# T5-bias attention with a maxout FFN: the values' load waits for the bias row's store, the second pass of batch 0 reuses the first pass's tiles and puts scores ahead of AV, the first FFN chunk runs weight by weight, and all loads are issued in written order

## The chip, the cores and the metric

The kernel runs on one core of one Trainium2 chip. The time is device microseconds of that core, the median over several runs. The core has five engines that run side by side: TensorE (PE, matmuls; its weight loads are shown as PEld), VectorE (DVE), ScalarE (ACT), GpSimd (POOL) and SyncE (SP). Sixteen DMA engines move data. In this kernel SP and ACT issue some transfers and POOL issues the rest; every transfer that changes f32 to bf16 on its way is POOL's.

## The reference

Two stages in sequence. Shapes: 8 batches, 8 heads, 576 positions, head size 64; model width 512, FFN width 768.

```python
scores = scale * q @ k.T                       # per batch and head, 576 x 576
scores = scores + bias_table[bucket(|i - j|)]  # 32 buckets, distances above 128 share one
attn   = exp(scores - max) / sum
x      = (attn @ v) laid out as 4608 tokens x 512
h      = maximum(maximum(x @ w1, x @ w2), x @ w3)
out    = h @ w_out                             # 4608 x 512, f32
```

## The kernel before

**Tiles.** Positions are four key tiles of 128 (`KT`) and a tail of 64. Heads go in pairs `hp` (four pairs). For a pair, `visit(qT, kT, e4, c)` makes the scores of 256 queries (`c` is 0 or 1) against all four key tiles: two PSUM tiles `sc` (two buffers of `ps_s`, L528), eight matmuls, and two `exp` on ACT (L522) of 128x1024 each into `e4`. `left_keys` (tile `sct`) and `left_queries` (tile `scq`) make the scores of the tail into `el`. The bias enters as a factor exp(bias): `times_band` (L516) multiplies `e4` on DVE by a band `hank`; `times_bandt` and `times_band_left` do the same for `el`. `attend(b, hp, e4, el, half)` multiplies with the values (`vx`, `vt`) into the PSUM tile `a` and gives back `quotients`, a reciprocal and a product on DVE (L608, L609) that write `x_sb`.

**The bias band.** `spread_bias` (L278) spreads the 32-entry table to a row per head with one matmul, takes exp on ACT, and stores the row to DRAM (`w_dr`, L287, queue of ACT). `load_hank` (L293, queue of SP) reads it back 128 times, one element further per partition, which gives the band. It waits for the store.

**Loads.** Batch 0 comes partly through f32 staging (`load_32`, `k32`, `q32`, queues of SP and ACT, cast by `cast_keys`), the rest from POOL (`load_main` L143, `load_tail` L160). Values are loaded by `load_v`. Then come the three weights `w_bf` (L660), the q and k of batch 1 in a packed form (`load_packed` L205, rearranged by `spread_packed` L210), the values of batch 1, `wo_bf` (L674), and `load_qk(2)` (L167). From batch 2 on q and k are turned by DMA transposes on SP (`transposes`, L447), handed out one position tile at a time by `next(crossbar)`; batches 0 and 1 are turned by PE (`first_transposes`, `more_transposes`, `second_transposes`).

**Order.** `inorder` fixes an instruction's place among those of its engine. Matmuls, DVE's work and SP's transfers are so fixed; POOL's loads are only from batch 3 on (`in_turn`, L133). PE runs through what is written, so an instruction that waits holds up all matmuls behind it.

**Batch 0 in two passes.** The first pass (L688) makes the scores of queries 0 to 255 for the four pairs; `late` collects the `attend` calls. The second pass (L719) makes those of queries 256 to 511 into new `e4` and `el` tiles, and between them takes attends from `late` (`next_late`). From batch 1 on (L768) each pair makes two visits, each followed by one attend of earlier work and by FFN work.

**FFN.** `add_ffn` cuts a chunk of tokens into portions, which `fill(target)` puts between the attention's matmuls: whole portions while their sum is at most `target`, and always one at least. A portion's number counts units of one matmul of 512 columns: 4 for a product of 128 FFN columns with one weight (`first`, `second`, `third` for w1, w2, w3), 6 for an `output` of 128 tokens. Tokens 0 to 255 and 256 to 511 are two small chunks, the rest chunks of 512. `x_transposes` (PE and ACT) bring batch 0's `x_sb` to `xT`, which the FFN reads; later batches use a DMA transpose (L619). A last output of a chunk (`rest`) is joined to the next chunk's first portion.

Of the kernel before, what the change touches and what calls it, by code (L numbers as in the profile page):

```python
# [39 lines left out]
def kernel(  # L40
# [77 lines left out]
    def constants(i):  # L118
        inorder(nc.vector.memset(ktail[i][:], 0.0))
        if i == 0:  # L120
            inorder(nc.vector.memset(qtail[i][:], 0.0))
        inorder(nc.vector.memset(vt[i][:], 0.0))
        inorder(nc.vector.memset(vx[i][:, :, :, D:AW], 1.0))
        for par in range(2):
            inorder(nc.vector.memset(vt[i][64 * par : 64 * par + 64, :, par, D:AW], 1.0))
# [7 lines left out]
    def in_turn(b, load):  # L133
        return inorder(load) if b > 2 else load

    def load_main(src, b, h0, h1, dst, t0=0, t1=KT):
        x = main_part(src, b)
        if h1 - h0 < KT:
            for h in range(h0, h1):
                nc.gpsimd.dma_start(out=dst[:, :, h, :], in_=x[:, :, h, :])  # L140
        else:
            for t in range(t0, t1):
                in_turn(b, nc.gpsimd.dma_start(out=dst[:, t, h0:h1, :], in_=x[:, t, h0:h1, :]))  # L143

# [16 lines left out]

    def load_qk(b, behind=None):

        loads = []
        for t in range(KT):
            for src, dst in zip((q, k), batch[b]):
                loads.append(in_turn(b, nc.gpsimd.dma_start(out=dst[:, t], in_=main_part(src, b)[:, t])))  # L167
        for src, dst in ((q, q_diag), (k, k_diag)):
            for par in range(2):
                load = nc.gpsimd.dma_start(out=dst(b, par, 0, H), in_=tail_part(src, b, 0, H, par))  # L170
                loads.append(in_turn(b, load))
        if behind:
            for load in loads:
                tc.add_manual_dep(
                    load.ins, behind.ins.name,
                    mybir.DependencyInfo(mybir.DependencyClass.Sync, mybir.DependencyReason.DATA),
                    reason="these loads go behind the result's transposes",
                )

    def load_v(b, h0, h1):  # L180
        load_main(v, b, h0, h1, vx[b % 2][:, :, :, 0:D])
        load_tail(v, b, h0, h1, v_diag)

# [36 lines left out]
    nc.gpsimd.dma_start(out=table[:], in_=bias_table)  # L220
    ident = const.tile([P, P], BF16, name="ident")
    make_identity(nc, ident[:])
    load_32(k, 0, k32, nc.scalar)
    load_32(k, 1, k32, nc.scalar)
    for h in range(2, KT):
        load_32(q, h, q32, nc.scalar, 2)
    nc.scalar.preload_act_table_set("natural_log_exp_and_others")
    for h in range(2):
        load_32(q, h, q32, nc.sync, 2)
    for h in range(2, H):  # L230
        load_32(k, h, k32, nc.sync)
# [6 lines left out]
    nc.gpsimd.iota(ids[:, 0:NW], pattern=[[1, NW]], base=0, channel_multiplier=0)  # L238
    nc.gpsimd.iota(ids[:, NW:], pattern=[[0, 1]], base=0, channel_multiplier=1)
# [4 lines left out]
    inorder(nc.vector.memset(qtail[1][:], 0.0))  # L244
# [13 lines left out]
    constants(1)  # L258
# [4 lines left out]
    load_v(0, 0, H)  # L263
# [8 lines left out]
    for _ in range(8):  # L272
        mm(warm[:, 0:CH], lhsT=zeros[:, 0:P], rhs=zeros[:])

    act_copy(batch[0][0][:, 0:2, 0:2, :], q32[:, :, 0:2, :])
    w_sb = stage.tile([H, WL], BF16, name="w_sb")

    def spread_bias():  # L278
        spread = ps_a.tile([H, NW], F32, tag="a", name="spread")
        mm(spread[:], lhsT=table[:], rhs=pick[:, 0:NW])  # L280
        negc = stage.tile([H, 1], F32, name="negc")
        inorder(nc.vector.tensor_scalar(
            out=negc[:], in0=spread[:, HALF:], scalar1=-1.0, scalar2=None, op0=ALU.mult,
        ))
        for out_, in_ in ((w_sb[:, HALF:], spread[:]), (w_sb[:, 0:HALF], spread[:, HALF:0:-1])):
            inorder(nc.scalar.activation(out=out_, in_=in_, func=ACTF.Exp, bias=negc[:]))
        inorder(nc.scalar.dma_start(out=w_dr[:], in_=w_sb[:]))  # L287
# [27 lines left out]
    def ffn(t0, nt, last):  # L315
# [13 lines left out]

        def bank(name):  # L330
            return ps_f.tile([P, CH], F32, tag="ff", name=name)

        def first(fb):
            ps0 = ps_a.tile([P, CH], F32, tag="a", name="ps0") if last else bank("ps0")
            product(ps0, fb, 0)
            st[fb]["m0"] = ffnw.tile([P, CH], BF16, tag="m0", name="m0")
            nc.scalar.activation(out=st[fb]["m0"][:], in_=ps0, func=ACTF.Copy)  # L337

        def second(fb):
            ps1 = ps_s.tile([P, 2 * CH], F32, tag="sc", name="ps1")[:, 0:CH] if last else bank("ps1")  # L340
            product(ps1, fb, 1)
            m = st[fb]["m"] = ffnw.tile([P, CH], BF16, tag="m", name="m")
            inorder(nc.vector.tensor_tensor(out=m[:], in0=ps1, in1=st[fb]["m0"][:], op=ALU.max))  # L343

        def third(fb):
            ps2 = bank("ps2")
            product(ps2, fb, 2)
            inorder(nc.vector.tensor_tensor(  # L348
                out=hT[:, fb * CH : fb * CH + CH], in0=ps2, in1=st[fb]["m"][:], op=ALU.max
            ))  # L350
# [36 lines left out]
        if per == 1:  # L387
            portions = [[f[0], m[0]]]
            for fb in range(1, n_fb):
                portions.append([g[fb - 1], f[fb], m[fb]])  # L390
            portions.append([g[-1], (0, None), o[0]])
        else:
            portions = []
            for fb in range(n_fb):
                portions += [[f[fb]], [m[fb], g[fb]]]
            portions.append(o[:1])
        if len(o) > 2:
            portions.append(o[1:3])
        return portions, o[-1:]

    pending, rest, stores = [], [], []
# [6 lines left out]
    def add_ffn(t0, nt, last=False):  # L408
        portions, left = ffn(t0, nt, last)
        portions[0] = rest + portions[0]  # L410
        rest[:] = left
        pending.extend((sum(n for n, _ in p), [fn for _, fn in p]) for p in portions)
# [237 lines left out]
    cast_keys(0)  # L650
    spread_bias()
    first_transposes(0)
    for h0 in (0, KT):
        load_hank(h0, h0 + KT)
# [3 lines left out]
    for i, wk in enumerate((moe_w1, moe_w2, moe_w3)):  # L658
        wb = const.tile([P, DCH, d_ff], BF16, name=f"w{i}_bf")
        nc.gpsimd.dma_start(out=wb[:], in_=wk.rearrange("(c p) f -> p c f", p=P))  # L660
        w_bf.append(wb)
    batch[1] = load_tiles()
    wo_bf = const.tile([P, FCH, d_model], BF16, name="wo_bf")

    def load_second():
# [6 lines left out]
        spread_packed(0, nc.gpsimd)  # L672
        load_v(1, 0, H)
        nc.gpsimd.dma_start(out=wo_bf[:], in_=moe_w_out.rearrange("(c p) m -> p c m", p=P))  # L674

    def bands(hp):
        for t in range(KT):
            times_band(hp, first_e[hp], t, 0, QS, inorder)
# [7 lines left out]
    first_e, lefts = [], []  # L686
    x_sb[0] = x_tile()
    for hp in range(HP):  # L688
        qT, kT = (x[:, hp, :] for x in qk[0])
        e4, el = e_tiles()  # L690
        first_e.append(e4)
        visit(qT, kT, e4, 0, (lambda: first_transposes(hp + 1)) if 0 < hp < HP - 1 else None)
        if hp == HP - 1:
            more_transposes(0)
        if hp == 0:
# [5 lines left out]
        if hp == HP - 1:  # L701
            bands(0)
            bands(1)
# [14 lines left out]

    for hp in range(HP):  # L719
        qT, kT = (x[:, hp, :] for x in qk[0])  # L720
        e4, el = e_tiles()
        visit(qT, kT, e4, 1, (lambda: more_transposes(hp + 1)) if hp + 1 < HP else None)
        if hp == 0:
            bands(HP - 2)
            bands(HP - 1)
        if hp == 1:
            x_transposes(0, 0)
        if hp == 2:
            x_transposes(2, 0)
            x_transposes(3, 0)  # L730
            add_ffn(0, QS)
        quotients = next_late()
# [7 lines left out]
        def late_bands():  # L740
            for t in range(KT):
                times_band(hp, e4, t, QS, QM, inorder)

        if hp < 2:
            quotients()
            keys()
            if hp == 1:
                x_transposes(1, 0)
            quotients = next_late()
            queries()  # L750
            quotients()
            if hp == 0:
                make_bandt()
            late_bands()
            products(hp, el)
        else:
            if hp == HP - 1:
                batch[2] = load_tiles()
                load_qk(2)
                x_transposes(0, 1)  # L760
            quotients()
            late_bands()
            fill(8, keys, queries, *([lambda: second_transposes(qk[1], 0)] if hp == HP - 1 else []))
            products(hp, el)
        late.append(lambda hp=hp, e4=e4, el=el: attend(0, hp, e4, el, 1))

    turned = [lambda hp=hp: x_transposes(hp, 1) for hp in range(1, HP)]
    for b, hp in [(b, hp) for b in range(1, B) for hp in range(HP)]:  # L768
# [19 lines left out]
        if turned:  # L788
            turned.pop(0)()
# [14 lines left out]
        if turned:  # L804
            turned.pop(0)()
# [5 lines left out]
        if hp == 1:  # L811
# [62 lines left out]
```

The softmax here doesn't subtract the row's maximum and nothing guards it: scores larger than these inputs give would overflow.

## Time and profile before

| | |
|---|---|
| median of 6 runs | 326.43 us (323.98 to 326.67) |
| the profiled execution's own time | 326.29 us |
| its span in the profile | 324.5 us |
| busy, share of the span | PE 307.2 us (95%), DVE 215.9 us (67%), ACT 201.9 us (62%), POOL 112.6 us (35%) |
| granted TensorE clock, mean | 0.989 |
| stretch 16.40 to 20.80 us | PE busy 0.02 of 4.40 us |
| stretch 20.80 to 25.80 us | PE busy 4.99 of 5.00 us, clock 0.50 |
| batch 1's matmuls, 38.0 to 66.5 us | PE busy 27.81, ACT 24.29, DVE 22.54 of 28.50 us |
| batch 4's matmuls, 130.9 to 164.8 us | PE busy 33.58 of 33.90 us |

The span begins with the first and ends with the last instruction; the run's time is 1.8 us longer. Busy time of PE is modelled from pipelined matmuls, so gaps of a tenth of a microsecond don't show. L94 is the helper that issues every matmul, and L110 and L107 are the helpers for copies on DVE and ACT, so those groups are told apart by their tiles. For a DMA the profile has the time at which an engine issued it and the time from issue to landing.

### The profile page before, as it was taken

The numbers are of one execution on the slowest core, as the hardware profiler recorded it, in microseconds if no ns is written. First come the engines' busy times: TensorE is split into PE (matmuls) and PEld (weight loads), VectorE is DVE, ScalarE is ACT, GpSimd is POOL, SyncE is SP. The second block draws the span as 40 slices with busy tenths as digits, with TensorE's granted clock in tenths as the row PEclk, the third lists the DMA queues.
The fourth block names the chain that finished last, engine by engine and source line by source line (L and its number), as shares of the span: only waits on it lengthen the run. The fifth ranks groups of instructions, "written<-read, shape, count | busy, mean of one in ns | idle before, by whom it ended". The sixth has DMA issues, their size and how long they took to land.

```text
span 324.5 us, 7978 instructions
## 1 busy us (share of the span) xinstructions
PE 307.2 (95%) x3191; PEld 176.0 (54%) x3232; DVE 215.9 (67%) x537; ACT 201.9 (62%) x274; POOL 112.6 (35%) x151
## 2 busy tenths in 40 slices
PE   7747999999999999999999999999999999999995
PEld 2335776776545555555555555555555554444442
DVE  6466978777676766676667766777667675454452
ACT  3938898898676667766777677667776651121221
POOL 8941977209747761195009610500000000000000
PEclk9969999999999999999999999999999999999999
DMA  9999999959999999999989999996032003301103
GB/s 168 177 207 198 150 161 141 166 128 126 179 167 152 156 177 174 125 123 168 202 81 122 168 209 87 104 210 115 1 71 101 34 3 75 130 0 65 67 0 129
DMA packets 165541, 40.72 MB, mean 125 GB/s; under 512 B 155384, under 2 KB 161024, under 8 KB 165504
## 3 DMA queue, kind: packets, MB, share of 16 engines
q0 software_dynamic: 103904, 16.66, 75.7%
q1 hardware_dynamic: 59840, 23.08, 39.3%
q10 hardware_dynamic: 1760, 0.47, 0.6%
q8 instruction: 25, 0.41, 0.5%
q14 instruction: 12, 0.10, 0.1%
HBM read 35.39 MB, written 9.45 MB: 138 GB/s over the span
## 4 chain that ended last, share of the span: by engine, by line
PE 81%; DMA 6%; ACT 5%; POOL 3%; issue 2%; DVE 2%; SPq 0%; POOLq 0%; ACTq 0%
PE ps L94 39%; PE a L94 14%; PE pso L94 13%; PE sc L94 9%; ACT e L522 4%; DMA kT<-k_sb 3%; PE sct L94 2%; DMA vt<-in_v_dram 2%; PE scq L94 2%; POOL vx L143 1%; POOL q_sb L143 1%; PE tp L97 1%; DMA out_dram<-osb 1%; ACT el L522 1%; DVE e L516 0%
## 5 line engine op out<-in xcount | busy, mean ns | idle before, releaser
L94 PE MATMUL ps<-xT,w_bf 128*128 128x512 bf16 (+1 forms) x692 | 152.5, 357 | 1.5
L522 ACT ACTIVATE e<-sc 128x1024 bf16<-128x1024 f32 x128 | 124.3, 1026 | 25.0 <-PE sc L94 24.4
L94 PEld LDWEIGHTS <-w_bf 128*128 128x128 bf16 x720 | 65.6, 98 | 56.8 <-issue 1.5
L516 DVE TENSOR_TENSOR e<-e,hank 128x512 bf16<-128x512 bf16 (+2 forms) x136 | 59.7, 467 | 27.6 <-ACT e L522 24.9
L337 ACT ACTIVATE m<-ps 128x512 bf16<-128x512 f32 x54 | 32.3, 598 | 65.7 <-PE ps L94 63.3
L343 DVE TENSOR_TENSOR m<-ps,m 128x512 bf16<-128x512 f32 x54 | 37.3, 690 | 46.0 <-ACT el L522 24.6
L94 PEld LDWEIGHTS <-kT 64*128 64x128 bf16 (+1 forms) x704 | 35.5, 95 | 39.4 <-issue 22.7
L94 PE MATMUL pso<-wo_bf,hT 128*128 128x512 bf16 (+2 forms) x209 | 50.2, 373 | 0.7
L94 PE MATMUL a<-vx,e 128*128 128x65 bf16 x1024 | 46.1, 195 | 0.0
L94 PE MATMUL a<-vt,el 128*128 128x130 bf16 (+1 forms) x192 | 40.1, 216 | 4.4 <-DMA vt<-in_v_dram 4.4
L94 PE MATMUL sc<-qT,kT 64*128 64x256 bf16 x512 | 41.1, 274 | 2.7 <-DVE kT L110 1.0
L94 PEld LDWEIGHTS <-e 128*128 128x128 bf16 x1024 | 41.8, 99 | 1.0 <-issue 0.2
L143 POOL DMA_DIRECT2D vx<-in_v_dram x32 | 28.4, 896 | 38.2 <-PE a L94 33.8
L348 DVE TENSOR_TENSOR hT<-ps,m 128x512 bf16<-128x512 f32 x54 | 37.0, 685 | 5.1 <-PE ps L94 3.3
L609 DVE TENSOR_TENSOR x_sb<-a,rd 128x256 bf16<-128x256 f32 (+1 forms) x64 | 31.4, 491 | 2.2
L94 PEld LDWEIGHTS <-el 128*128 128x128 bf16 x448 | 24.3, 97 | 15.7 <-issue 10.1
L110 DVE COPY osb<-pso 128x512 f32<-128x512 f32 (+1 forms) x33 | 22.7, 687 | 13.4 <-PE pso L94 10.1
L94 PEld LDWEIGHTS <-hT 128*128 128x128 bf16 x222 | 20.2, 98 | 20.6 <-DVE hT L348 0.4
L167 POOL DMA_DIRECT2D q_sb<-in_q_dram x24 | 22.1, 922 | 16.5 <-DVE x_sb L609 14.3
L522 ACT ACTIVATE el<-sct 128x640 bf16<-128x640 f32 (+2 forms) x36 | 23.2, 646 | 5.7 <-PE sct L94 5.1
L167 POOL DMA_DIRECT2D k_sb<-in_k_dram x24 | 22.0, 917 | 7.5 <-DMA vx<-in_v_dram 5.9
L522 ACT ACTIVATE el<-scq 128x512 bf16<-128x512 f32 x32 | 19.0, 595 | 6.6 <-PE scq L94 6.6
(69 smaller groups left out, 168.8 us busy)
## 6 DMA issues: line engine op xcount, KB each, us to landing
out_dram<-osb SPq DMA_DIRECT2D x35, 256.0 KB, 3.2
vx<-in_v_dram POOLq DMA_DIRECT2D x32, 128.0 KB, 6.3
q_sb<-in_q_dram POOLq DMA_DIRECT2D x26, 128.0 KB, 8.6
k_sb<-in_k_dram POOLq DMA_DIRECT2D x24, 128.0 KB, 8.8
w_bf<-in_moe_w_dram POOLq DMA_DIRECT2D x3, 768.0 KB, 14.1
xT<-in_k_dram SPq DMA_DIRECT2D x6, 128.0 KB, 4.4
hank<-w_dr SPq DMA_DIRECT2D x2, 384.0 KB, 7.4
wo_bf<-in_moe_w_out_dram POOLq DMA_DIRECT2D x1, 768.0 KB, 8.4
```

The costliest lines, as they stand in the source:

```text
L94: inorder(nc.tensor.matmul(*args, **kw))
L97: inorder(nc.tensor.transpose(*args))
L110: return inorder(nc.vector.tensor_copy(out_, in_))
L143: in_turn(b, nc.gpsimd.dma_start(out=dst[:, t, h0:h1, :], in_=x[:, t, h0:h1, :]))
L167: loads.append(in_turn(b, nc.gpsimd.dma_start(out=dst[:, t], in_=main_part(src, b)[:, t])))
L337: nc.scalar.activation(out=st[fb]["m0"][:], in_=ps0, func=ACTF.Copy)
L343: inorder(nc.vector.tensor_tensor(out=m[:], in0=ps1, in1=st[fb]["m0"][:], op=ALU.max))
L348: inorder(nc.vector.tensor_tensor(out=hT[:, fb * CH : fb * CH + CH], in0=ps2, in1=st[fb]["m"][:], op=ALU.max))
L516: put(nc.vector.tensor_tensor(out=e4[:, t, :, lo:hi], in0=e4[:, t, :, lo:hi], in1=hank[:, 2 * hp : 2 * hp + 2, c0:c1][:, :, ::-1], op=ALU. ...
L522: nc.scalar.activation(out=out_, in_=in_, func=ACTF.Exp, scale=inv_sqrt_d)
L609: divided[b, hp, half] = inorder(nc.vector.tensor_tensor(out=x_sb[b][:, 2 * half : 2 * half + n, P * hp : P * hp + P].rearrange("p t (h d) ...
```

## The change

- `load_v(0)` waits for the store of the bias row (`go_behind`), and stands behind `spread_bias` in POOL's order.
- All loads of POOL are in written order. The written order is now: q and k of batch 0, values of batch 0, w1, first packed q and k of batch 1 with their tails, w2, `spread_packed(0)`, the other packed q and k, values of batch 1, w3, `w_out`.
- The start: the bias table goes over SP's queue instead of POOL's, the identity is made by two POOL instructions behind the `iota`s, two clears move from DVE to POOL, the first casts are all DVE's and take one head each, 6 warming matmuls stand where 8 did and one more after the first transposes, and `constants(1)` moves behind the third pair of the first pass.
- The second pass of batch 0 uses `e4` and `el` of the first. Pairs 0 and 1 have all their scores (visit, keys, queries) ahead of the first attends, with extra `keep_warm` matmuls; the bands of the first pass move from its end into pairs 0 and 1 of the second. Attends start at the end of pair 1. Three attends of the second half are made in the second pass, where two were.
- The small FFN chunks go by weights: all products with w1, then with w2; those with w3 and the outputs of tokens 0 to 255 follow the second small chunk's w1 and w2 products. Every product is a portion of its own. The intermediate maxima are kept in `hT`. `fill(4)` is called three times in the second pass where `fill(8)` was called twice.
- In batch 1 the second small chunk is added in pair 0, where it was pair 1; `x_transposes` are taken two at a time.

```diff
+            return [
                 in_turn(b, nc.gpsimd.dma_start(out=dst[:, t, h0:h1, :], in_=x[:, t, h0:h1, :]))
+                for t in range(t0, t1)
+            ]
...
+    def go_behind(loads, other, reason):
+        for load in loads:
+            tc.add_manual_dep(load.ins, other.ins.name, ...)
...
+    def load_v(b, h0, h1, behind=None):
+        loads = load_main(v, b, h0, h1, vx[b % 2][:, :, :, 0:D])
         load_tail(v, b, h0, h1, v_diag)
+        go_behind(loads if behind else [], behind, "the bias row is on its way to memory alone")
...
-    nc.gpsimd.dma_start(out=table[:], in_=bias_table)
...
+    inorder(nc.sync.dma_start(out=table[:], in_=bias_table))
...
+    inorder(nc.gpsimd.memset(ident[:], 0.0))
+    inorder(nc.gpsimd.affine_select(out=ident[:], in_=ident[:], ...
+    for x in (qtail, ktail):
+        inorder(nc.gpsimd.memset(x[1][:], 0.0))
...
-            st[fb]["m0"] = ffnw.tile([P, CH], BF16, tag="m0", name="m0")
+            st[fb]["m0"] = part(fb) if t0 < CH else ffnw.tile([P, CH], BF16, tag="m0", name="m0")[:]
...
+        if per > 1:
+            return [[x] for x in f + m], [[x] for x in g + o]
...
+        if t0 == 0:
+            third[:] = left
+        elif t0 < CH:
+            portions += third + left[:-1]
+            rest[:] = left[-1]
+        else:
+            portions[0] = rest + portions[0]
+            rest[:] = left[0]
...
-    cast_keys(0)
-    spread_bias()
+    dve_copy(batch[0][1][:, :, 0, :], k32[:, :, 0, :])
+    dve_copy(batch[0][0][:, 0:2, 0:2, :], q32[:, :, 0:2, :])
+    dve_copy(batch[0][1][:, :, 1, :], k32[:, :, 1, :])
+    row = spread_bias()
+    load_v(0, 0, H, row)
...
+                load_weights(1, moe_w2)
+                spread_packed(0, nc.gpsimd)
         load_v(1, 0, H)
+        load_weights(2, moe_w3)
...
         if hp == HP - 1:
             more_transposes(0)
+            more_transposes(1)
...
+        e4, el = first[hp]
+        visit(qT, kT, e4, 1, (lambda: more_transposes(hp + 2)) if hp + 2 < HP else None)
...
+        if hp < 2:
+            bands(2 * hp)
+            bands(2 * hp + 1)
+            keys()
+            keep_warm()
+            queries()
+            keep_warm()
         if hp == 1:
+            next_late()()
+            next_late()()
         if hp == 2:
+            for half in range(2):
+                next_late()()
+                x_transposes(half, 0)
+            keys()
+            queries()
             x_transposes(2, 0)
             x_transposes(3, 0)
             add_ffn(0, QS)
+            make_bandt()
+            late_bands(0)
+            fill(4)
+        if hp == 3:
+            batch[2] = load_tiles()
+            load_qk(2)
+            late_bands(1)
+            next_late()()
+            fill(4, keys)
             queries()
+            late_bands(2)
+            next_late()()
+            fill(4, lambda: second_transposes(qk[1], 0))
         late.append(lambda hp=hp, e4=e4, el=el: attend(0, hp, e4, el, 1))
+    late_bands(3)
+    next_late()()
...
-        if hp == 1:
+        if hp == (b > 1):
             add_ffn((b - 1) * CH if b > 1 else QS, CH if b > 1 else QS)
```

## The prediction

> **What bounds the kernel now.** I read the stretches first, then PE's waits, then the chain, then SP's and POOL's timelines. The stretches (microseconds from A to B; busy time and count per engine, clock, DMA share, GB/s):
>
> ```profile
> 9.00:12.00 3.00, 2.55 (x30) 1.24 (x27) 1.53 (x5) 2.82 (x6) 3.00 (x4) 1.00 2.34 151
> 16.40:20.80 4.40, 0.02 (x2) 0.02 (x1) 3.34 (x12) 1.69 (x2) 1.67 (x3) 0.79 1.59 200
> 20.80:25.80 5.00, 4.99 (x58) 3.62 (x59) 3.40 (x14) 2.35 (x4) 2.19 (x4) 0.50 1.16 210
> 33.00:35.00 2.00, 2.00 (x44) 1.68 (x43) 1.97 (x6) 1.94 (x4) 1.97 (x4) 1.00 0.97 119
> 38.00:66.50 28.50, 27.81 (x414) 21.09 (x417) 22.54 (x62) 24.29 (x36) 16.43 (x22) 1.00 1.97 161
> 66.50:97.10 30.60, 30.03 (x371) 19.07 (x374) 22.41 (x57) 23.80 (x32) 18.20 (x23) 1.00 1.54 144
> 130.90:164.80 33.90, 33.58 (x364) 18.75 (x370) 23.66 (x56) 23.64 (x31) 14.28 (x18) 1.00 1.73 152
> ```
>
> From batch 2 on PE sets the pace. Batch 4 has 96 FFN units of 0.216 us (eight matmuls of 256 columns, four units, stand with 0.87 us in the chain), 20.7 us, which leaves 13.2 us for its attention. Time is lost only before about 66 us. Where, the waits and the chain say:
>
> ```profile
> PE a L94 <- DMA vt<-in_v_dram: 4.4, 1, 4.4
> ...
> 12.19 0.58 POOL vt L160
> 12.77 7.90 DMA vt<-in_v_dram
> 20.68 0.14 issue
> 20.81 1.25 PE a L94 x18
> ```
>
> The first attend stands ahead of the second pass's work and waits 4.4 us for the values; then TensorE runs at half clock for 5 us, in which the 58 matmuls would have needed about half the time. The second pass starts late by some 4.4 + 2 us. The other thing to see is when batch 2's operands come. SP's timeline, SP's longest wait, PE's timeline and POOL's:
>
> ```profile
> 48.77 1.29 SPq L447 DMA_TRANSPOSE qT<-q_sb  x1
> ...
> 58.52 1.22 SPq L447 DMA_TRANSPOSE kT<-k_sb  x1
> ...
> SPq L447 <- DMA q_sb<-in_q_dram: 40.4, 4, 37.2
> ...
> 66.47 0.61 PE L94 MATMUL sc<-qT,kT 64*128 64x256 bf16 x8
> ...
> 28.48 0.83 POOL L205 DMA_DIRECT2D xT<-in_k_dram  x1 [3.19 <-DMA w_bf<-in_moe_w_dram]
> 32.44 0.82 POOL L205 DMA_DIRECT2D xT<-in_q_dram  x1 [3.13 <-DMA w_bf<-in_moe_w_dram]
> ...
> 39.30 0.89 POOL L674 DMA_DIRECT2D wo_bf<-in_moe_w_out_dram  x1
> 40.12 0.95 POOL L167 DMA_DIRECT2D q_sb<-in_q_dram  x1
> ```
>
> SP sits from 11.4 to 48.77 until the first q of batch 2 has landed, and then issues ten transposes back to back. The last key tile's (58.52) takes 7.3 us to land: 65.8. PE reads it in the second half of the visit at 66.47, at about 66.7. So batch 2 can start only about 0.9 us earlier than it does, however early PE gets there, unless its loads come earlier. They stand last in POOL's line: batch 0, V, three weights, batch 1, `w_out`, then they.
>
> **What the Trainium skill says.** "TensorE: Matmul & The Clock Gate", section "The HAM clock gate": an idle window returns the array to half clock. The trace agrees: idle from 16.4, half clock until 25.8. "DMA: Bandwidth & Descriptors", section "Queues, rings and completion order": each DMA engine takes turns between the queues that have work. The trace agrees: the band's read on SP's queue (issued 10.47, landed 17.3) and the values on POOL's share the engines. Same page, section "Anatomy of one DMA": a wait happens on the issuing sequencer before dispatch. So V's new wait holds all POOL work behind it; no run shows that yet.
>
> **The change, part by part.**
>
> *Start.* The table landed 3.6 us after its issue at 1.29, 4.9, and the spread began at 5.02. On SP it is third, issued about 1.7; with the neighbours' 2.5 us it lands at 4.2 to 4.5. No `constants(1)` (0.84 us) stands ahead of the first casts, but those wait for k's second head (1.28 + 3.5 = 4.8). I take 0.6 us earlier for row and first scores. POOL loses a DMA issue (0.66) and gains two clears of 128x512, unseen there: 0.2 us each (scaled down from DVE's 0.27) to 0.8 (POOL's copy of this size is 0.74). Taking 0.5, its loads start within 0.4 us of 2.80. The key tails already made PE wait at 9.86, so the first pass gains little: it ends on ACT at 18.0 (before: 18.09).
>
> *V behind the row.* The row left at 7.35 and landed at 10.4, 3.1 us later; 0.6 earlier is about 9.7, against V's first issue at 8.55. Six issues (4 x 0.9 + 2 x 0.65 = 4.9 us) follow. Queued behind on POOL: w1 and everything else. The q and k loads fill the DMA to about 11, so I put the hole at 1.1 us (0 to 2): V lands near 21.8, the band near 16.7.
>
> *Scores ahead of AV.* Pairs 0 and 1 of the second pass cost ACT 2 x (2.0 + 0.45 + 0.6) = 6.1 us, from 18.0 to 24, so V is needed only at about 23; there the 4.4 us go. The clock dip then costs nothing, as ACT sets the pace. Whole second pass: ACT 12.2, four `xT` copies 1.4, three w1 copies 1.8, half of `second_transposes` 0.8, together 16.2 us. DVE: twelve band products 3.7, their second-half twins 3.8, tails 2.0, seven quotients 4.5, `bandt` 1.0, copies 1.5, together 16.5 us from 16.7. Neither is free to follow the other exactly; with 2 us of friction it ends at 36. Before it ended at 37.98, with one attend (1.0 us) fewer. The four new `keep_warm` matmuls (0.22 us each, 0.9 us on PE) are hidden by ACT's pace; were PE the slower engine there, they would cost that.
>
> *Batch 1.* PE: attention 13.2, less one attend 1.0, three `second_transposes` 1.65, four `xT` turns 0.5, 60 FFN units 13.0, together 27.3 us; before, 52 units and 26.5 us took 28.5. I take 28.5: PE is ready for batch 2 at 64.5, 2 us earlier than before.
>
> *Loads in order.* The same bytes stand ahead of batch 2's loads. Against: the hole of 1.1 us. For: before, the DMA ran thin twice because POOL issued late, in 33.0 to 35.0 (119 GB/s, against 190 before it) and in 41 to 42 (93 GB/s against 175): 0.75 + 0.5 us. The first came of the packed load that waited for w3 (32.44); in the new order packed loads stand ahead of w3 and w2's 3.9 us cover `spread_packed`'s 1.4. So batch 2's loads move by -0.2 us, (-1.5 to +1.5), and batch 2 can start 0.9 + 0.2 = 1.1 us earlier. PE has 2 us. Of the two the later counts: **-1.0 us**, the rest becomes a new wait at batch 2.
>
> *FFN ahead.* I played the portions through both versions. Units done at the start of batch 2: 64 before, 72 after; at the start of batch 3: 140 and 152; the difference of 12 then stays until the attention ends. Batch 2 carries four more (+0.86 us), and its end has 0.38 us of DMA wait less, as PE waited that long at 97.12 for keys. Behind batch 3 there are 12 fewer: **-2.6 us**.
>
> *Tokens of batch 1.* In batch 2 the first 512-token chunk starts one visit earlier: at about 78.3 on the old clock, where it started at 81.27. It needs the fourth of five DMA transposes that SP issues from 69.30 to 77.30; with 5.3 us to landing that is 79.2. **+0.8 us** (0 to 1.5).
>
> Moves without cost: maxima kept in `hT` (the same writes); the small chunk's w2 and w3 (their first use is behind 36 and 48 us, they land by about 32 and 44); shared `e4` tiles (the queries differ).
>
> Sum: -1.0 + 0.86 - 0.38 - 2.6 + 0.8 = -2.3 us. The profiled run took 326.29, so 324.0 (span 322.2); it lies at the median of 326.43, and I say **324.1 us**.
>
> **Rivals.**
>
> 1. *Batch 2's loads come with PE, early.* The holes at 33 and 41 us close and V's wait makes none: loads 2 us earlier, PE 3 us earlier if the second pass has no friction. Then -2.9 instead of -1.0: 322.2. For: DMA is then full all through. Against: ACT and DVE both nearly full.
> 2. *The operands land when they did.* Hole of 2 us, nothing gained later: batch 2 starts at 66.5, and with 1.5 us for tokens the sum is 0 + 0.48 - 2.6 + 1.5 = -0.6: 325.8, no change.
> 3. *The new wait halves the clock (slower).* PE waits 2 to 4 us at batch 2's first visit as it did for V. The half clock after that wait lasted 6.8 us in the trace's clock record, 1.8 of it idle. In batch 2 PE sets the pace and nothing hides it: up to 6.8/2 = 3.4 us. With rival 2: -0.6 + 3.4 = +2.8: 329.2. It decides once batch 2 starts no earlier than before and the halved stretch is over 4.5 us long. For: the same idle did it at 16.4. Against: PE's wait would be shorter than those 4.4 us by my sum.
>
> That V's wait on the row leaves the band no earlier, because k and q fill the DMA until 11 anyway, is possible and changes the sum by less than 0.5 us.
>
> **How the numbers follow.** A difference under 0.5% (1.6 us) can't be told from none. My case 0.45, own range 322.8 to 325.4; rival 1 0.18; rival 2 0.20; rival 3 0.17. Faster is below 324.8: 0.36 of mine and all of rival 1, 0.54. Same: 0.09 of mine, 0.17 of rival 2, 0.03 of rival 3, 0.29. Slower: 0.03 of rival 2 and 0.14 of rival 3, 0.17. For 8 in 10 the range reaches from 321.0 into rival 3, to 328.6.
>
> **What would show it.** Right: no wait of attend for V over 1 us; batch 1's first visit near 36; a PE wait of 0.5 to 2 us for DMA transposes at batch 2's first visit near 65.5; the later visits some 2 us earlier than before. Wrong: V landing after 24, with PE idle behind it; the first q of batch 2 landing before 47 or after 50; a clock of half after 60 us; a PE wait for `xT` over 1.5 us near 78.

## The result, and the profile after

The changed kernel takes 329.03 us (median of 18 runs, 325.77 to 334.24) against 326.3 for the kernel before (median of 39 runs here, where the six above gave 326.43): ratio 1.0083, 95% interval 1.0060 to 1.0106. It is slower by 2.7 us; 324.1 was predicted, and the range of 321.0 to 328.6 ends below the median. One of the 18 runs, that of 334.24 us at a mean clock of 0.983, was in a slower state and is left out of the ratio; without it the median is 328.64. The profiled execution took 328.12 us with a span of 326.3 (before 326.29 and 324.5), so its 1.8 us are what the trace can explain; the medians lie 0.5 to 0.9 further apart.

The stretches of the kernel after, in the columns used before (A:B and length; busy time and count of PE, PEld, DVE, ACT, POOL; clock, DMA share, GB/s):

```profile
16.40:20.80 4.40, 2.73 (x27) 1.51 (x29) 2.37 (x9) 4.31 (x8) 3.52 (x6) 1.00 1.96 174
20.80:25.80 5.00, 4.11 (x84) 3.17 (x81) 3.44 (x12) 3.77 (x6) 1.83 (x3) 1.00 1.43 194
38.00:66.50 28.50, 26.95 (x359) 20.42 (x361) 21.34 (x56) 23.07 (x35) 13.42 (x17) 1.00 1.78 175
66.50:97.10 30.60, 28.83 (x350) 17.61 (x354) 21.14 (x53) 21.85 (x27) 18.30 (x23) 1.00 1.59 138
130.90:164.80 33.90, 32.72 (x352) 17.96 (x355) 22.67 (x54) 22.58 (x29) 14.26 (x18) 1.00 1.44 138
```

The hole at 16.4 and the half clock behind it are gone in this execution: the first two rows have clock 1.00 and 111 matmuls where there were 60. The later rows pay for it: PE is idle for 1.55, 1.77 and 1.18 us in these stretches, where before it was for 0.69, 0.57 and 0.32. What PE waits for, by the operation released and its releaser (total us, times, longest):

```profile
PE ps L93 <- ACT xT L106: 2.2, 3, 0.9
...
PE ps L93 <- DMA xT<-x_sb: 1.2, 1, 1.2
PE sc L93 <- DMA kT<-k_sb: 1.0, 1, 1.0
PE sct L93 <- DMA kT<-ktail: 0.9, 1, 0.9
```

There is no wait for V at all. In its place stand three waits for DMA transposes, tokens (`x_sb`) and operands (`k_sb`, `ktail`), and waits of the FFN's first matmuls (`ps`) for ACT's copy of turned tokens. PE's timeline has the places (start, duration, and in brackets the idle time before it and what ended it):

```profile
66.69 0.61 PE L93 MATMUL sc<-qT,kT 64*128 64x256 bf16 x8
...
79.95 0.59 PE L93 MATMUL ps<-xT,w_bf 128*128 128x512 bf16 x2 [1.18 <-DMA xT<-x_sb]
...
136.94 0.45 PE L93 MATMUL sct<-qT,kT 128*128 128x512 bf16 x2 [0.92 <-DMA kT<-ktail]
...
169.43 0.28 PE L93 MATMUL sc<-qT,kT 64*128 64x256 bf16 x2 [0.98 <-DMA kT<-k_sb]
```

The first scores of each batch, read in both PE timelines, make a running account. "Like for like" takes off what the after kernel has already done more by then: one attend (1.0 us) at batch 1, 8 FFN units (1.73) at batch 2, 12 (2.6) from batch 3.

| first visit of | before | after | difference | like for like | predicted visit |
|---|---|---|---|---|---|
| batch 1 | 37.98 | 35.58 | -2.4 | -3.4 | 36 |
| batch 2 | 66.47 | 66.69 | +0.2 | -1.5 | 65.5 |
| batch 3 | 96.24 | 98.95 | +2.7 | +0.1 | 96.9 |
| batch 4 | 130.80 | 132.84 | +2.0 | -0.6 | 131.1 |
| batch 5 | 164.68 | 167.95 | +3.3 | +0.7 | 165.0 |
| batch 6 | 198.56 | 202.99 | +4.4 | +1.8 | 198.8 |
| end | 324.5 | 326.3 | +1.8 | +1.8 | 322.2 |

The predicted visits follow from the prediction's terms (batch 3: 96.24 - 1.0 + 0.86 + 0.8; then - 0.38). The gain of 3.4 us is there at batch 1 and then goes: 1.9 in batch 1, 1.6 in batch 2, and, where the prediction saw nothing left to happen, 1.2 in each of batches 4 and 5; batch 3 gives 0.7 back. From batch 6 on the two kernels take equally long, but for the 12 units that the kernel after has done already.

Each column is one execution. Kernels below whose edits come into play only later, from 62 us on, reached batch 1 at 34.95 to 36.26 us and batch 2 at 66.06 to 67.36, so the shares of batches 1 and 2 are known to about 0.7 us. Those of batches 4 and 5 are firmer: without waits they take 33.88 us each, in the kernel before and in edited ones below, and here they took 35.11 and 35.04.

SP's timeline of the kernel after, at batch 2's operands and in batch 4 (start, duration, DMAs issued):

```profile
48.10 1.30 SPq L459 DMA_TRANSPOSE qT<-q_sb  x1
...
58.29 2.78 SPq L459 DMA_TRANSPOSE kT<-k_sb  x1
...
135.33 10.18 SPq L631 DMA_TRANSPOSE xT<-x_sb  x5
145.61 0.52 SPq L391 DMA_DIRECT2D out_dram<-osb  x1
146.24 1.30 SPq L459 DMA_TRANSPOSE qT<-q_sb  x1
...
164.67 1.71 SPq L459 DMA_TRANSPOSE kT<-ktail  x1
```

The same stretch of the kernel before:

```profile
133.29 8.21 SPq L619 DMA_TRANSPOSE xT<-x_sb  x5
141.61 1.28 SPq L447 DMA_TRANSPOSE qT<-q_sb  x1
142.99 1.28 SPq L447 DMA_TRANSPOSE kT<-k_sb  x1
144.36 0.54 SPq L379 DMA_DIRECT2D out_dram<-osb  x1
...
158.43 1.81 SPq L447 DMA_TRANSPOSE kT<-ktail  x1
```

In both, SP issues these nineteen DMAs (five token transposes, four stores, ten operand transposes) with hardly a gap. Before they took 26.95 us (133.29 to 160.24), after 31.05 (135.33 to 166.38); the five token transposes have 2.0 of the 4.1 us more. The first store, which stood behind the first q and k, now stands ahead of them, and the others have moved up by one pair of transposes as well. The change of this order is a side effect: the FFN's lead of 12 units moves the outputs one visit forward, and `store_outputs()` is called ahead of that visit's transposes.

POOL's timeline of the kernel after has the values' new wait:

```profile
11.62 3.53 POOL L142 DMA_DIRECT2D vx<-in_v_dram  x4 [3.08 <-DMA w_dr<-w_sb]
```

POOL stood 3.08 us for the row's store; batch 2's first q was still turned 0.7 us earlier than before (48.10 against 48.77).

### The profile page after: what moved, and what is told of

It reads as the page before. It is cut to its first block, busy times and chain, and to the rows that moved or that the text cites. A ratio compares the mean times of both kernels' runs of the same rounds, so it can differ in the third digit from the quotient of the medians.

```text
span 326.3 us, 7978 instructions
## 1 busy us (share of the span) xinstructions
PE 308.0 (94%) x3191; PEld 176.0 (54%) x3235; DVE 215.0 (66%) x537; ACT 201.9 (62%) x273; POOL 112.9 (35%) x152
## 4 chain that ended last, share of the span: by engine, by line
PE 70%; DMA 12%; ACT 7%; SPq 5%; DVE 2%; issue 2%; POOL 1%; ACTq 0%; POOLq 0%
PE ps L93 34%; PE a L93 11%; PE pso L93 11%; PE sc L93 8%; ACT e L534 5%; SPq L459 4%; DMA k_sb<-in_k_dram 3%; DMA kT<-k_sb 3%; DMA kT<-ktail 2%; PE sct L93 2%; PE scq L93 2%; DMA xT<-x_sb 2%; DMA xT<-in_k_dram 1%; PE tp L96 1%; DVE e L528 1%
## 5 line engine op out<-in xcount | busy, mean ns | idle before, releaser
L349 ACT ACTIVATE m<-ps 128x512 bf16<-128x512 f32 x48 | 28.7, 597 | 65.5 <-PE ps L93 65.5
L355 DVE TENSOR_TENSOR m<-ps,m 128x512 bf16<-128x512 f32 x48 | 33.2, 691 | 47.2 <-ACT el L534 27.7
L93 PE MATMUL a<-vx,e 128*128 128x65 bf16 x1024 | 44.9, 193 | 0.0
L93 PEld LDWEIGHTS <-e 128*128 128x128 bf16 x1024 | 40.7, 97 | 1.0
L360 DVE TENSOR_TENSOR hT<-ps,m 128x512 bf16<-128x512 f32 x48 | 32.9, 685 | 4.4 <-PE ps L93 3.0
```

The costliest lines, as they stand in the source:

```text
L93: inorder(nc.tensor.matmul(*args, **kw))
L349: nc.scalar.activation(out=st[fb]["m0"], in_=ps0, func=ACTF.Copy)
L355: inorder(nc.vector.tensor_tensor(out=m, in0=ps1, in1=st[fb]["m0"], op=ALU.max))
L360: inorder(nc.vector.tensor_tensor(out=part(fb), in0=ps2, in1=st[fb]["m"], op=ALU.max))
```

## The experiments

In the expectations, T is this account: the gain is lost at PE's first visits because the operands' own chain (POOL's loads, SP's transposes and stores in order) did not get earlier or got longer, and in batch 1 because tokens are turned two at a time. R is the rival that the loss is made in batches 0 to 2 by the new order, and that the later waits only show it. W is the rival that the values' wait, with all of POOL's work behind it, is what costs.

**Stores on another queue.** The output stores of all but the last chunk are issued by ACT, so that SP has transposes alone. The same edit goes into the kernel before as its control.

```diff
-    inorder(nc.sync.dma_start(...))
+    inorder((nc.sync if last else nc.scalar).dma_start(...))
```

> The changed kernel, with the output stores of all chunks but the last ones issued from ACT's queue instead of SP's. Theory T (SP's chain of each batch, five token transposes, four stores, ten operand transposes and their landing, takes as long as PE's 33.9 us, so what the FFN lead gained is waited away at batches 4 and 5): SP's chain gets about 2 us shorter per batch, PE's waits for operands at batches 4 and 5 (0.9 and 1.0 us, with what follows them 2.4 us) go, time about 326.5 to 327.0, ratio to the kernel before 1.000 to 1.003. Rival R (the loss is made in batches 0 to 2 by the new order on PE and ACT; the later waits only show it): as the changed kernel, 1.007 to 1.009.

> The kernel before, with the same edit. T: its operands arrive with 0 to 1.3 us to spare and PE waits only 0.4 us at batch 3, so at most 0.5 us is won: 0.998 to 1.001. R: no difference, 0.999 to 1.001.

Measured: 379.12 us, ratio 1.1653 (1.1597 to 1.1709), and for the kernel before 361.4, ratio 1.1024 (1.0954 to 1.1094). ACT's waits in the edited kernel after, and then PE's, say why:

```profile
ACT m L349 <- DMA qT<-q_sb: 39.2, 4, 11.6
...
ACT m L349 <- DMA kT<-k_sb: 5.7, 1, 5.7
...
PE sc L93 <- ACT el L534: 39.9, 9, 9.5
```

The wait is named at the instruction behind the store: `m` is a maxout operation and needs no operand of the attention. A store issued on ACT's queue stood until transposes that SP had issued landed, 44.9 us in five stalls, and the exps queued behind them on ACT; PE then waited 39.9 us for `el`. This brought a bigger wait than the one it was to remove, so it says nothing on T. Whether the stores wait by something that the program has been given for it, or in the chip, is not settled.

**The stores behind the transposes, on SP.** The order alone is changed, on the same queue, again with the control.

```diff
         visit(qT, kT, e4, 0)
-        store_outputs()
         ...                       # crossbar transposes of this visit
+        store_outputs()
```

(and the same at the second visit)

> The changed kernel, with the output stores of a visit written behind the operand transposes of that visit in SP's order, not ahead of them. T, in the form that the stores ahead of the transposes are what makes the chain too long at batches 4 and 5: the waits there go, 2.4 us faster than the changed kernel, 0.998 to 1.002. R: as the changed kernel, 1.007 to 1.010.

> The kernel before with the same edit. T: it hardly waits there, so 0.998 to 1.001. R: 0.999 to 1.001.

Measured: 326.7 us, ratio 1.0016 (0.9993 to 1.0038), 2.3 us under the changed kernel, with intervals that do not meet; the kernel before takes 325.72, ratio 0.9986 (0.9964 to 1.0008), no change that can be told. So the order costs the kernel after about 2.3 us (2.2 by the ratios) and the kernel before little or nothing, as T expected of both. SP's timeline of the edited kernel after:

```profile
136.61 8.94 SPq L631 DMA_TRANSPOSE xT<-x_sb  x5
145.66 1.20 SPq L459 DMA_TRANSPOSE qT<-q_sb  x1
...
148.27 0.53 SPq L391 DMA_DIRECT2D out_dram<-osb  x1
...
163.75 1.49 SPq L459 DMA_TRANSPOSE kT<-ktail  x1
```

The chain is 28.63 us here (136.61 to 165.24), 2.4 shorter, and PE waits neither in batch 4 nor in batch 5. The trace must not be read for more: this profiled execution took 328.58 us, 1.9 over its median, had 1.8 us of wait for tokens in batch 2 and 1.3 for keys in batch 6, where SP's chain of batch 5 was 29.4 us again. Part of its time was lost far ahead of the first moved store: the clock was half from 8 to 14 us, and batch 1 began at 36.26, the latest of the kernels with this beginning.

```profile
8.00:14.00 6.00, 5.39 (x35) 2.45 (x36) 2.71 (x8) 4.33 (x7) 2.84 (x4) 0.50 1.44 153
```

That the order matters is shown by the times; how much of the longer chain is order and how much is transposes that were slow to issue for another reason is not.

**The operands one visit earlier.** From batch 3 on the crossbar transposes begin at the first pair instead of the second.

```diff
-            if hp == 1:
+            if hp == 1 and b == 2:
                 crossbar = transposes(b + 1)
...
+        if b > 2 and hp == 0 and b + 1 < B:
+            crossbar = transposes(b + 1)
+            next(crossbar)
```

> The changed kernel, with the operand transposes of batches 4 to 7 starting one visit earlier (ahead of the second group of token transposes). T: the waits at batches 4 and 5 go, with 2.4 us; the lead of 12 FFN units is then kept to the end: 0.998 to 1.002. R: as the changed kernel, 1.007 to 1.010.

Measured: 327.41 us, ratio 1.0025 (1.0004 to 1.0046), 1.6 us under the changed kernel. The ratio is a little above what T expected (0.998 to 1.002) and well under R's. PE has no wait for keys left, and batches 4 and 5 begin 33.88 us apart, and 5 and 6 33.89:

```profile
132.29 0.61 PE L93 MATMUL sc<-qT,kT 64*128 64x256 bf16 x8
...
166.17 0.61 PE L93 MATMUL sc<-qT,kT 64*128 64x256 bf16 x8
...
200.06 0.61 PE L93 MATMUL sc<-qT,kT 64*128 64x256 bf16 x8
```

The profiled execution, at 329.27, had 3.0 us of wait for tokens (the longest 2.3), and the clock of 78 to 84 us was 0.83. The waits for operands are confirmed as a cost from a second side.

**Without the lead.** Chunks behind the first are added after the fill of the visit instead of ahead of it, which puts the outputs back where they fell before.

```diff
-        if hp == (b > 1):
-            add_ffn((b - 1) * CH if b > 1 else QS, CH if b > 1 else QS)
+        if b == 1 and hp == 0:
+            add_ffn(QS, QS)
...
+        if b > 1 and hp == 1:
+            add_ffn((b - 1) * CH, CH)
```

> The changed kernel, with each 512-token chunk added after the fill of its visit instead of before it. This takes back the visit by which the chunks start earlier (and the lead of 12 units at batch 3). T: the token wait of 1.2 us at batch 2 goes and PE reaches batch 3 some 3.5 us earlier, but waits there 2 us or more for the operands; from batch 3 on the stretches are as long as before; time 326.5 to 328, ratio 1.001 to 1.005. R: batch 2 starts as in the changed kernel, no new wait at batch 3 over 0.5 us, and the whole loses as much as it won, 1.006 to 1.010.

Measured: 327.62 us, ratio 1.0059 (1.0027 to 1.0091), between what T and R expected, and not to be told from the changed kernel's 1.0083. The trace has what T expected, one wait of 2.0 us for batch 3's keys:

```profile
98.15 0.28 PE L93 MATMUL sc<-qT,kT 64*128 64x256 bf16 x2 [1.99 <-DMA kT<-k_sb]
```

From batch 4 on it takes 33.88 us per batch with no further wait (132.02, 165.90, 199.78, 233.67). So giving up the lead of 2.6 us costs nothing that the measurement can tell: its waits eat it. SP's chains of batches 4 and 5 are short again, 27.32 and 26.05 us (31.05 and 29.50 in the changed kernel, 26.95 and 26.41 before). With the lead kept and only the stores moved they were 28.63 and 29.41, so the chain grows with the lead and not by the stores' order alone; why is open. That the time is over the kernel before's with the lead gone shows that batches 1 to 3 have their own loss, as R has it.

**Turning tokens, half on DVE.** Of the two token turns of a half visit in batch 1 the second is copied by DVE.

```diff
-    def x_transposes(hp, half):
+    def x_transposes(hp, half, copy=act_copy):
...
-    turned = [lambda hp=hp: x_transposes(hp, 1) for hp in range(HP)]
+    turned = [lambda hp=hp: x_transposes(hp, 1, dve_copy if hp % 2 else act_copy) for hp in range(HP)]
```

> The changed kernel, with the second of each two token turns in the first pair of batch 1 copied by DVE instead of ACT. Both theories: PE's waits for ACT's copies there (0.8 and 0.5 us) shrink, the pair takes 8 to 8.7 us instead of 9.7. T: PE then waits for batch 2's operands, which land no earlier than about 66.3; the time stays within 0.6 us of the changed kernel, 1.006 to 1.010. R: the gain of 1 to 1.6 us stays, 1.003 to 1.005.

Measured: 328.35 us, ratio 1.0089 (1.0058 to 1.0120): no faster than the changed kernel. But pair 0 of batch 1 takes 8.03 us (35.46 to 43.49) instead of 9.68. PE's waits in this kernel:

```profile
PE sc L93 <- DMA kT<-k_sb: 3.1, 2, 2.0
...
PE ps L93 <- DMA xT<-x_sb: 1.5, 1, 1.5
```

The 1.65 us are gained where T puts them and come back as waits for operands. ACT's copies were a loss, since the two turns hold both banks of `ps_f` until ACT, with the exps ahead of them, has copied; behind it stands the operands' landing, which the prediction called a floor. At batch 2 PE came at 64.92 and then stood for the last key tile:

```profile
67.40 0.28 PE L93 MATMUL sc<-qT,kT 64*128 64x256 bf16 x2 [1.98 <-DMA kT<-k_sb]
```

This floor is not a fixed time. The tile was issued at 57.76 and landed 9.6 us later; in the changed kernel it was issued at 58.29 and took 7.1 us, to 65.4, so there PE, at 66.69, didn't meet the floor at all.

**The values without their wait.**

```diff
-    load_v(0, 0, H, row)
+    load_v(0, 0, H)
```

> The changed kernel without the wait of batch 0's values for the row's store (same place in POOL's order). T: values and all later loads come 1 to 2 us earlier, batch 2's operands land about 1 us earlier, PE wins at most the 0.4 us that it waited there: 1.006 to 1.010, as the changed kernel. A third idea, W (the wait itself is what costs, through everything queued behind it on POOL): 1.5 to 3 us faster than the changed kernel, 1.000 to 1.004.

Measured: 329.08 us, ratio 1.0074 (1.0049 to 1.0099), where the changed kernel has 1.0083. V's first issue comes at 8.48 instead of 11.62, batch 2's first transpose at 47.31 instead of 48.10, its first visit at 66.03 instead of 66.69; by then the wait for tokens is 2.2 us. W falls: the part that stands first in the change's name costs nothing that the measurement can tell.

**Easing all the waits.** To the stores behind the transposes, a later start of batch 2's first 512-token chunk (one visit, at the end of the fill, with a bigger fill behind it that keeps the lead) is added; then the turns on DVE and the values without their wait; then `w_out`'s load behind the loads of batch 2; then the operands one visit earlier.

```diff
-        fill(rate, lambda: left_keys(hp, qT, kT, el, 0, S + 64))
+        fill(20 if (b, hp) == (2, 2) else rate, lambda: left_keys(hp, qT, kT, el, 0, S + 64))
...
-        if hp == (b > 1):
+        if (b, hp) == (2, 1):
+            pending.append((sum(n for n, _ in rest), [fn for _, fn in rest]))
+            rest[:] = []
+        elif hp == (b > 1):
...
+        if (b, hp) == (2, 1):
+            add_ffn(CH, CH)
```

> The run with the stores behind the operand transposes, and besides the first 512-token chunk starts one visit later (behind the fill of the second visit of pair 1 of batch 2; the next fill takes 20 units, so that the lead of 12 units is kept). T: the token wait of 1.2 to 2.3 us at batch 2 goes; of it 0.5 to 1.5 us stay won, the rest is waited for operands at batch 3 (they land near 97.5): 0.995 to 1.000. R (the wait is hidden behind another): as without the edit, 1.001 to 1.002.

> The same, with the DVE copies of every second token turn in batch 1 and without the values' wait for the row. T: batch 1 is then 1.6 us shorter and batch 2's operands land about 0.8 us earlier, so that some 0.5 to 1 us more than in the run above is won: 0.992 to 0.998. If batch 2's operands land no earlier, as the run above.

```diff
-        inorder(nc.gpsimd.dma_start(out=wo_bf[:], in_=moe_w_out.rearrange("(c p) m -> p c m", p=P)))
...
             load_qk(2)
+            inorder(nc.gpsimd.dma_start(out=wo_bf[:], in_=moe_w_out.rearrange("(c p) m -> p c m", p=P)))
```

> The last run's kernel with the load of w_out behind batch 2's q and k loads in POOL's order, where it stood ahead of them. If batch 2's start is set by the DMA line (the same bytes ahead of its loads, as the prediction had it), the operands land some 3 us earlier, PE's 2.1 us wait at batch 2's first visit and the half clock behind it go, and 1 to 2.5 us are won on the run before: 0.988 to 0.994. If they are set by SP's ten transposes alone, the wait stays and the time is as before, 0.994 to 0.998. If w_out is then late for the first outputs (near 57 us), a wait of PE for it shows there.

> The same, with the operand transposes of batches 4 to 7 starting one visit earlier. T: what waits for operands is left at batches 4 and 5 (0.2 us each in the run before) goes; 0 to 0.5 us better than the run above, unless the token transposes behind them come late again.

| kernel | us | ratio (95%) |
|---|---|---|
| changed | 329.03 | 1.0083 (1.0060 to 1.0106) |
| stores behind | 326.7 | 1.0016 (0.9993 to 1.0038) |
| and tokens later | 325.78 | 0.9995 (0.9969 to 1.0020) |
| and DVE turns, no wait of V | 324.57 | 0.9957 (0.9933 to 0.9981) |
| and `w_out` behind | 325.05 | 0.9967 (0.9942 to 0.9991) |
| and operands early | 326.44 | 1.0001 (0.9973 to 1.0030) |

With the waits eased the change is faster than the kernel before, by 0.43% or 1.4 us; this is the best kernel of the study, if by less than was predicted for the change as it stands. With the tokens later, PE waits 0.6 us for tokens and 1.1 for operands in all. The two turns and the wait of V, which moved nothing by themselves, come with 1.2 us once the waits behind them are eased; the two intervals overlap, so this is likely and not shown.

`w_out` behind the loads of batch 2 was a miss: the first transpose of batch 2 came at 44.00, 3.3 us earlier than in the run before it (47.25), but two of the key issues stretched to 3.09 and 3.28 us and the last key tail was issued at 60.40, only 0.5 us earlier (60.91); the time did not fall. The operands earlier on top, from which up to 0.5 us was expected, were a miss too: they put batch 4's first q and k ahead of three token transposes of batch 3, which SP issued from 104.73 to 109.44, and PE stood 2.44 us before an FFN matmul that reads tokens:

```profile
113.78 1.82 PE L93 MATMUL ps<-xT,w_bf 128*128 128x512 bf16 x4 [2.44 <-DVE e L528]
```

The profile puts this wait to an instruction of DVE that had ended earlier. The three transposes took about 8.7 us to land, and the first of them would be down at about 113.4, so I take the wait to be theirs. Neither order found more slack in this chain.

The kernel with all waits eased but `w_out` shows one more thing, in an execution 3 us over its median. PE's timeline at batch 2, and its stretch:

```profile
66.72 0.28 PE L93 MATMUL sc<-qT,kT 64*128 64x256 bf16 x2 [2.07 <-DMA kT<-k_sb]
```

```profile
68.00:72.00 4.00, 4.00 (x29) 2.59 (x27) 1.69 (x4) 1.02 (x3) 0.00 (x0) 0.64 0.33 68
```

After 2.07 us of waiting the clock falls to 0.64 of full, and PE, busy without a gap, gets through 29 matmuls in 4 us. A wait of that length does not always do it. The kernel with the turns on DVE alone has the same stretch behind its wait of 1.98 us, with more than twice the matmuls:

```profile
68.00:72.00 4.00, 4.00 (x70) 3.28 (x66) 2.36 (x6) 2.68 (x4) 0.00 (x0) 1.00 0.40 107
```

And these are the two microseconds behind a wait for tokens of 2.22 us (to 80.34, the values without their wait) and behind one of 2.34 (to 81.32, the operands earlier):

```profile
82.00:84.00 2.00, 2.00 (x32) 1.16 (x30) 0.89 (x3) 1.62 (x4) 0.90 (x1) 1.00 1.92 168
82.00:84.00 2.00, 2.00 (x8) 0.94 (x8) 0.00 (x0) 1.09 (x2) 1.54 (x3) 0.50 1.89 144
```

## Why the prediction was wrong

**Right.** The mechanism of the first half held. Attend waits for V no more, batch 1 was reached at 35.58 (36 was said), the clock of the profiled execution stayed whole, and the lead was 8 and then 12 units. The term *Tokens of batch 1* (+0.8, 0 to 1.5) measured 1.18. *Loads in order* lies in its range (first q 48.10 against 48.77 before, 0.7 us earlier where 0.2 was said), by some luck, since two terms under it failed. *Start* had the row 0.6 us earlier: the table landed at 4.9 as before, the row's store was issued at 7.12 against 6.82, 0.3 later, and the first pass ended its large exps at 19.5 and not at 18.0. And V's hole was 3.08 us and not 1.1: V's first issue came at 11.62 and not near 9.7. That wait was free, as the run without it shows.

**The step that failed** is *FFN ahead*: "the difference of 12 then stays until the attention ends", priced at -2.6 us. From batch 2 on I let PE set the pace and did not ask whether SP, which feeds it, could keep it. In batches 3 to 6 SP's round of nineteen DMAs took 25 to 29 us before and 26 to 31 after, and a key tail needs 7 to 8 us more from its issue to its landing. A round begins some 2.5 us into a batch, when the tokens are there, and the next batch needs the tail 2.9 us after its start, so with PE's 33.9 us per batch the room is about 34.3. Before, that just fitted: batch 4's tail was issued at 126.14, had landed by about 133.5 and was read at 133.68. After, it was issued at 128.95 and landed 7.9 us later, and PE stood for it until 136.94. The lead leaves this room as it is, but it changes SP's own order, and the round of batch 4 grew by 4.1 us. So 1.2 us each were waited away in batches 4 and 5, 2.4 of the 4.1 between 322.2 and 326.3. The stores behind the transposes bring back 2.3, the operands a visit earlier 1.6; giving up the lead costs nothing that can be told. The prediction followed its moved steps through the loads and through PE, not through the stores on SP's queue.

**The second miss** is *Batch 1*: "I take 28.5" measured 31.1. PE was ready at 66.5 and not at 64.5, and *Batch 1*'s -1.0 became +0.2: 1.2 of the 4.1. The sum of PE's own work (27.3) left out that two turns in one half take both banks of `ps_f`; 1.65 us of the 2.6 are shown by the copies on DVE, the rest is open. The floor itself, the last key tile's landing at 65.8 less 0.2, was also mis-sized, as the 7.3 us to landing were taken as fixed: in the changed kernel it lay at 65.4 and did not bind, and where PE came earlier, at 64.92 and 64.15, the tile landed 9.6 and 9.7 us after its issue and PE stood until 67.40 and 66.72. So taking the turns' loss away alone gained nothing.

The rest is small: batch 2 lost 0.8 more than predicted (0.4 of it tokens), and 0.3 came back in batch 3. Of the 4.1 us, then, 2.4 fall to T and about 2 to what R names, batches 1 and 2.

**The rivals.** None named SP's order. Rival 2, a late second batch, came nearest in its place (66.69, it said 66.5) and would have given 325.8. Rival 3, the one on the slower side, did not happen in the changed kernel's trace: its clock is whole to the end. Its mechanism is real, though, as three of the edited kernels show, after waits of 2.07, 2.34 and 2.44 us, while others kept the clock after 1.98, 1.99 and 2.22. The trace is also one of the executions with a whole clock. Of the 18 executions that count, profiled one included, nine had a mean clock of 0.989 to 0.995, and their median is 329.62 us, against 328.12 for the nine at 0.998 or more. So low clocks probably enter the 0.5 to 0.9 us by which the medians lie further apart than the profiled executions. This is not shown: where the clock fell in those nine is not on record, it need not be at batch 2 (it was at 8 to 14 us in one edited kernel, at 18 to 22 in two), and the kernel with the tokens later has no such difference. In the forecast of chances, slower had too little because the only way there was drawn through the clock.

## What to carry to other kernels

When work of the pacing engine is moved forward, draw the second chain that feeds it: if an issue queue's round, with landing, is as long as the engine's own, whatever lengthens that round is waited for at the next handover. Here the lead lengthened it, in part by the four stores that it put ahead on the queue, and its gain was waited away. Where a queue is shared, try stores behind the next round's loads, and start the consumers of late transfers later. A wait removed in a stretch with a floor behind it must be counted only down to the floor, and the floor needs a range of its own, since landing times differ (here 7.1 to 9.7 us for the same tile).

## What the runs showed of the hardware that was not expected

- An output store issued on ACT's queue stood until DMA transposes issued by SP had landed: 44.9 us in five stalls, up to 11.6 us each. Where this wait is made is open, as said above. Moving the stores from one queue to another cost 50 us in the kernel after and 35 in the kernel before.
- The issue of one DMA transpose on SP is not a constant: 1.2 us mostly, 3.1 and 3.3 for two of the key tiles when SP issued them earlier, at 51 and 56 us; five token transposes took 8.0 to 10.2 us before and after. Nor is its landing: batch 2's last key tile took 7.1 us from its issue in the changed kernel and 9.7 in the one with all waits eased.
- A PE wait of 2.07 us was followed by a clock of 0.64 over the next 4 us, and one of 2.34 by 0.50 at 82 to 84 us, but one of 2.22 left it at 1.00. The Trainium skill, "TensorE: Matmul & The Clock Gate", section "The HAM clock gate", says that the clock halves after an idle window of about 3.4 us; here shorter waits sufficed in some executions and not in others. So the length of a wait of 2 us alone did not tell whether the clock would fall.
- The same kernel's first wait for V differs between executions: 4.4 us in the kernel before as profiled, 2.0 in the same kernel with the stores behind, which differs only later. That execution reached batch 1 at 36.60, where the profiled kernel before reached it at 37.98; the gain from removing the wait differs by as much.
